# Two feed-forward groups of seven blocks in place of four, and halves of a P V step only where nothing else of TensorE is due shortly

## The chip, the cores and the metric

The kernel runs on one core of a Trainium2 chip. The metric is device time in microseconds (us) of one execution; lower is better. Times given as a median are over the runs shown; a profile is of one execution of its own.

## The reference

A block of a transformer, for 2048 positions of width 512: attention with 32 query heads of 16 dimensions and one key and value head, a feed-forward part of width 1792 with SiLU, and a sigmoid gate that mixes them.

```python
def _A_ref(x, wq, wk, wv, wo):          # H = 32 heads, Dh = 16, S = 2048
    q = (x @ wq).reshape(B, S, H, Dh)   # per head
    k, v = x @ wk, x @ wv               # one head for all
    p = softmax(einsum("bhqd,bkd->bhqk", q, k) * Dh ** -0.5)
    return einsum("bhqk,bkd->bhqd", p, v).reshape(B, S, H * Dh) @ wo
def _B_ref(x, w1, w2):                  # F = 1792
    return silu(x @ w1) @ w2
g = sigmoid((x * gate_w).sum(-1, keepdims=True))
return g * a + (1 - g) * b
```

All inputs are float32, and the kernel keeps nearly that precision: a float32 operand is split into a 16-bit upper and a 16-bit lower part, and a product is made of three passes (upper by upper, upper by lower, lower by upper).

## The kernel before, in words

**Steps.** The queries are worked in 4 chunks `c` of 512 positions and 4 blocks `o` of 8 heads: 16 rounds. A round has 32 steps, one for each 64 keys, so there are 512 steps. A step has two score tiles `S` of 128 x 1024 (TensorE, `scores`, L1225), each turned into probabilities by one exponential of ScalarE (`exponential`, L1231) into a buffer `P` (the rows call it `xs` where the buffer was part of the input's). There are two score buffers, so a score can begin when the exponential before the last one has ended. After the two exponentials the step is multiplied by the values (`pv`, L1262) in one of these ways:
- in 16-bit parts, "A" and "B": VectorE first makes the two lower parts of the step (`low`, L1237, one for each half of the tile, into `L` or `raw`), and TensorE makes a bfloat16 pass and a float16 pass;
- natively in float32, "W": one whole step without VectorE;
- natively in halves, "N" and then "M": the same work as W, in two pieces of 256 columns that other work can stand between.

**The rest of TensorE's work** is one stream of outputs (`Stream`, L851): the blocks of the feed-forward's first product (`ffn_h`, tile `pm` from `xs,w1s`, 12 passes each, 14 blocks for each chunk), its second product (`ffn_o`, from `w2s,H`), the queries (`q_block`, from `xs,wqs`) and the attention's output product (`out_proj`, from `wo_s,O`). TensorE is used as two row halves of 64: an output `new` goes through the lower rows while the output before it, `cur`, goes through the upper rows. Both write their own PSUM bank, of which there are two (`pM`). One such pairing lasts as many passes as the longer of the two and is called a turn here. When `cur` has ended it is evicted (`evict`): the first product through a tanh of ScalarE (L906) and two operations of VectorE (L909, L922), the second product by adding it to the accumulator of its 128 positions (`add_out`, L828 for the first, L830 for the further ones). The next turn waits until that bank is free (`self.last.free`).

**Groups.** The 14 blocks of a chunk are worked in groups (`GROUPS`): the outputs of the second product are made for each group by itself, so each of the 16 tiles of 128 positions gets one addition for each group. The groups of the first three chunks are 4, 3, 4, 3 with the row halves taking different spans (`spans`, `order`), so that 12 passes meet 12 and 9 meet 9; the last chunk has 4, 4, 4, 2, where a turn of 12 meets one of 6. Blocks of the next group are put between the outputs of this one (`mixed`).

**Order.** `attention` writes the order of all engines while the program is built. A planner (`advance`, `pe_next`, `act_next`, `dve_next`) keeps a clock for TensorE, ScalarE and VectorE, with fixed costs (`PASS` 0.216, `HALF` 0.435, `EXP` 0.905 and others), and takes for each engine what is ready and has the lowest priority number. For TensorE a score has 0, a P V step 4 (3 for A and B, 1 when the backlog of steps is long), the stream 2 while it is behind a steady pace and 5 when it is ahead. A whole native step is only taken where the next score would still be in time for ScalarE; where it isn't, but a half would be, the step is begun in halves:

```python
if HALVES and r is not None and s not in left_of and max(r, now["PE"]) > most:
    fits, kind = most + HALF, "NM"
```

VectorE takes a step's lower parts if it can end both within `ROOM` of the first exponential. On the chip each engine follows the order written, and waits only where an operand isn't there.

**Other parts.** Before the loop lies a prologue (keys, first queries, the first pieces of the weights), and the weights are loaded and split in `pieces`, one every 5.6 us by the planner. The last three steps of the last round are made by halves of the queries (L1218, L1250), and four products with the last part of `wo` end the kernel (L1715).

Of the kernel before, what the change touches and what calls it, by code (L numbers as in the profile page):

```python
# [36 lines left out]
HALVES = True  # L37
PAIRS = 3
XUSE = "PPP "
GROUPS = (4, 3, 4, 3), (4, 3, 4, 3), (4, 3, 4, 3), (4, 4, 4, 2)  # L40
UNEVEN = [sum(g) == 14 and g[:3] == (4, 3, 4) for g in GROUPS]
# [15 lines left out]
def kernel(  # L57
# [99 lines left out]
    pieces = [(w1, 0, a) for a in range(KD)]  # L157
    for g in range(len(GF)):
        if g + 1 < len(GF):
            pieces += [(w1, g + 1, a) for a in range(KD)]  # L160
        if g == 0:
            pieces += [(wq, 0, a) for a in range(2)]
        pieces += [(w2, g, a) for a in range(GF[g])]
# [645 lines left out]
    def attention(ctx, pO, scale_of, t_scale, shifts, split_pieces, chores, q_todo, early, gates_, v_bank):  # L809
# [29 lines left out]
        class Out:  # L839


            def __init__(self, terms, ready, kind, evict, add=None, upper=None):
                self.kind, self.evict, self.ready, self.add = kind, evict, ready, add
                parts = lambda terms: [(l, r, i, j) for l, r in terms for i, j in ((0, 0), (0, 1), (1, 0))]
                self.mm = parts(terms)
                self.mm_hi = self.mm if upper is None else parts(upper)
                self.free = self.wait = None
# [16 lines left out]


# [27 lines left out]
        def weights(w, k):  # L893
            _, f0, n_f = blocks[k]
            return all(split_pieces.ready(w, g) for g in range(len(GF)) if f0 < sum(GF[:g + 1]) and f0 + n_f > sum(GF[:g]))

        def ffn_h(k, f):
            c, f0, n_f = blocks[k]
            fa = f0 + f
            f0 = fa * 128  # L900

            def tangent(o, t):
                x_used(c, t)
                e = wp.tile([128, 512], F32, name="e", bufs=EB)
                e_left[0] -= 1
                nc.scalar.activation(e, o.bank, AF.Tanh, scale=t_scale)  # L906
# [21 lines left out]
            return Out([(lambda i, b, m, n=32, kt=kt: w1s[b, i, kt, f0 + m:f0 + m + n],  # L928
                         lambda j, b, kt=kt: xs[b, c, j, kt]) for kt in range(KD)],
                       lambda: 0.0 if weights(w1, k) else None, "h",  # L930
                       lambda o, t: tanhs.append((t, lambda t: tangent(o, t))))

        def spans(k, t):

            c, f0, n = blocks[k]
            g = k % 4
            if not UNEVEN[c]:
                return range(f0, f0 + n), range(f0, f0 + n)
            a, b = ((0, 4, 7, 11, 14), (0, 3, 7, 10, 14))[::1 if t % 2 == 0 else -1]
            return range(a[g], a[g + 1]), range(b[g], b[g + 1])  # L940

        def order(k):

            return (1, 0, 3, 2) if UNEVEN[blocks[k][0]] and k % 2 else (0, 1, 2, 3)

        def ffn_o(k, t):
            c, f0, n_f = blocks[k]
            spans_ = spans(k, t)
            used = sorted({*spans_[0], *spans_[1]})

            def ready():
                if not weights(w2, k) or any((c, f) not in h_done for f in used):
                    return None
                return max(h_done[c, f] for f in used)

            def evict(o, when):
                if t == order(k)[-1]:
                    kept = {f for n in range(4) for q in spans(k + 1, n) for f in q} if k + 1 < len(blocks) and blocks[k + 1][0] == c else set()
                    h_more([Hs.pop((c, f)) for f in range(f0 + n_f) if (c, f) in Hs and f not in kept], when)
                o.added(when)  # L960

            terms = [[(lambda i, b, m, n=32, f=f: Hs[c, f][b, i, t * 128 + m:t * 128 + m + n],
                       lambda j, b, f=f: w2s[b, j, f]) for f in q] for q in spans_]
            return made_out(terms[0], ready, "o", evict, c, t, g1, terms[1])

        def made_out(terms, ready, kind, evict, c, t, gate, upper=None):
            o = Out(terms, ready, kind, evict, upper=upper)
            o.add = lambda: add_out(c, t, o.bank, gate)
            return o
# [82 lines left out]
        def outs():  # L1052

            def mixed(k):
                hs = [lambda f=f: ffn_h(k, f) for f in range(blocks[k][2])] if k < len(blocks) else []
                os_ = [lambda t=t: ffn_o(k - 1, t) for t in order(k - 1)] if k else []
                at_once = 0 if not k else 2 if UNEVEN[blocks[k - 1][0]] else 4 if blocks[k - 1][2] < NF else 1
                for _ in range(len(hs) if k == len(blocks) - 1 else LEAD - 1):
                    if hs:
                        yield hs.pop(0)  # L1060
                while len(hs) > 1 or os_:
                    if len(hs) > 1:
                        yield hs.pop(0)
                    if queue:
                        yield lambda n=queue.pop(0): q_block(n)
                    for _ in range(at_once):
                        if os_:
                            while k and blocks[k - 1][0] > asked[0]:
                                yield None
                            left[0] -= 1  # L1070
                            yield os_.pop(0)
                yield from hs

            for n in early:
                yield q_block(n)
            for k in range(len(blocks) + 1):
                for make in mixed(k):
                    if make is None:
                        yield urgent.pop(0)() if urgent else None
                        continue  # L1080
                    while k == len(blocks) and any((blocks[k - 1][0], f) not in h_done for f in range(14)):
                        yield urgent.pop(0)() if urgent else None
                    yield make()
                    while urgent:
                        yield urgent.pop(0)()
            while True:
                yield urgent.pop(0)() if urgent else None
# [4 lines left out]
        class Stream:  # L1092


            def __init__(self):
                self.new = self.cur = self.last = self.next = None
                self.n = self.i = self.others = self.passes = 0
                self.paired = False

            def ready(self):  # L1100

                if self.i < self.n:
                    return self.new.wait if self.new and not self.i else 0.0
# [4 lines left out]
                if self.last and self.last.free is None:  # L1108
                    return None
                r = self.next.ready()  # L1110
                return None if r is None else max(r, self.last.free if self.last else 0.0)

            def turn(self, t):

                if self.cur and not (self.next and self.paired):
# [3 lines left out]
                if self.new:  # L1119
                    self.new.bank, self.new.wait = pM.tile([128, 512], F32, name="pm"), 0.0  # L1120
                    if any(b[3] <= t for b in bounds):
                        bound(self.new, t + PASS + LATE)
                        return True

            def go(self, t):
                if self.i == self.n and self.turn(t):
                    return
                for m in range(4):
                    if self.new and self.i < len(self.new.mm):
                        self.new.product(self.new.mm[self.i], lo, m, self.i == 0, False)  # L1130
                    k = self.i - self.n + len(self.cur.mm_hi) if self.cur else -1
                    if k >= 0:
                        self.cur.product(self.cur.mm_hi[k], hi_, m, False, self.i == self.n - 1)
                self.i += 1
                self.passes += 1
                if self.i == self.n:
                    self.paired = self.cur is not None
                    if self.cur:
                        self.cur.evict(self.cur, t + PASS + LATE)
                        self.last = self.cur  # L1140
# [435 lines left out]
        def pe_next():  # L1576
# [19 lines left out]
            ok = [x for x in cands if x[0] <= t + 0.03]  # L1596
            return min(ok, key=lambda x: x[1]) if ok else min(cands, key=lambda x: x[0], default=None)
# [90 lines left out]
        while head[0] < len(steps) or left[0] > 4 or tanhs or len(h_done) < sum(GF) * NCH:  # L1688
            advance()
# [75 lines left out]
```

## Time and profile before

| what | value |
|---|---|
| median of 3 runs | 1030.44 us (1029.58 to 1033.46) |
| profiled execution | 1030.14 us, its span 1028.4 us |
| TensorE busy | 1006.5 us (98%) |
| ScalarE busy | 992.3 us (96%) |
| VectorE busy | 924.5 us (90%) |
| GpSimd busy | 60.0 us (6%) |
| exponentials / low parts / additions L830 with `g` | 1024 / 490 / 48 |

A row of a timeline gives start, length, engine, line, operation, output and inputs, and how many instructions are merged in it. Matmuls are pipelined and a row's length reaches to the end of the last one, so the cost of a pass on TensorE is read from its start to the start of what follows. A pass is 8 matmuls, a native half or whole step shows as 16. A row of a group gives the count after the x, then busy time and mean length, then the idle time of the engine before it and what ended it.

### The profile page before, as it was taken

The numbers are of one execution on the slowest core, as the hardware profiler recorded it, in microseconds if no ns is written. First come the engines' busy times: TensorE is split into PE (matmuls) and PEld (weight loads), VectorE is DVE, ScalarE is ACT, GpSimd is POOL, SyncE is SP. The second block draws the span as 40 slices with busy tenths as digits, with TensorE's granted clock in tenths as the row PEclk, the third lists the DMA queues.
The fourth block names the chain that finished last, engine by engine and source line by source line (L and its number), as shares of the span: only waits on it lengthen the run. The fifth ranks groups of instructions, "written<-read, shape, count | busy, mean of one in ns | idle before, by whom it ended". The sixth has DMA issues, their size and how long they took to land.

```text
span 1028.4 us, 69785 instructions
## 1 busy us (share of the span) xinstructions
PE 1006.5 (98%) x32760; PEld 616.2 (60%) x32760; DVE 924.5 (90%) x1199; ACT 992.3 (96%) x1108; POOL 60.0 (6%) x138
## 2 busy tenths in 40 slices
PE   8999999999999999999999999999999999999996
PEld 6456565666655656565656556566666556565563
DVE  7888978989999999999999999899998989999893
ACT  5999999999999999999999999999999999999994
POOL 4101101100000000000000000000000000000000
PEclk9999999999999999999999999999999999999999
DMA  5123322311010111101011010100110110101001
GB/s 208 48 87 85 82 59 60 76 45 25 10 42 18 48 33 25 30 5 32 19 24 41 24 46 15 35 20 15 47 27 17 43 39 10 36 10 19 5 4 47
DMA packets 28115, 40.14 MB, mean 39 GB/s; under 512 B 5689, under 2 KB 19370, under 8 KB 27818
## 3 DMA queue, kind: packets, MB, share of 16 engines
q0 software_dynamic: 10656, 15.73, 7.4%
q1 hardware_dynamic: 16442, 19.27, 5.9%
q8 instruction: 258, 4.23, 1.8%
q10 hardware_dynamic: 720, 0.59, 0.2%
q14 instruction: 39, 0.32, 0.1%
HBM read 19.98 MB, written 8.25 MB: 27 GB/s over the span
## 4 chain that ended last, share of the span: by engine, by line
PE 83%; ACT 10%; DVE 3%; issue 3%; DMA 1%; SPq 0%; ACTq 0%
PE pm L851 32%; PE pv L1262 28%; PE S L1225 20%; ACT P L1231 7%; ACT xs L1231 2%; DVE L L1237 1%; ACT e L906 1%; PE pv L1250 1%; DMA xn<-in_A_x_dram 1%; PE pt L339 0%; DVE xs L132 0%; DVE e L909 0%; PE pv L518 0%; PE pm L436 0%; PE S L1218 0%
## 5 line engine op out<-in xcount | busy, mean ns | idle before, releaser
L1231 ACT ACTIVATE P<-S 128x1024 f32<-128x1024 f32 x770 | 737.5, 1077 | 10.5 <-PE S L1225 5.5
L1225 PE MATMUL S<-qb,KT 50*32 50x512 f16 x8096 | 483.4, 379 | 5.7 <-ACT P L1231 1.8
L1225 PEld LDWEIGHTS <-KT 50*32 50x32 f16 x8096 | 206.1, 90 | 189.1 <-issue 100.0
L1237 DVE TENSOR_TENSOR L<-P 128x1024 f16<-128x1024 f32 x227 | 271.5, 1217 | 20.7 <-ACT P L1231 19.6
L851 PE MATMUL pm<-xs,w1s 64*32 64x512 f16 x5376 | 274.8, 375 | 1.1 <-DVE e L909 0.8
L851 PE MATMUL pm<-w2s,H 64*32 64x512 f16 x5376 | 273.8, 375 | 1.3 <-DVE e L909 0.8
L1262 PE MATMUL pv<-P,VF 64*32 64x256 f32 (+1 forms) x5056 | 267.5, 450 | 0.3
L1231 ACT ACTIVATE xs<-S 128x1024 f32<-128x1024 f32 x254 | 253.6, 1080 | 2.1 <-PE S L1225 0.9
L851 PEld LDWEIGHTS <-w1s 64*32 64x32 f16 x5376 | 126.5, 93 | 44.2 <-issue 8.4
L851 PEld LDWEIGHTS <-H 64*32 64x32 f16 x5376 | 125.3, 93 | 44.0 <-issue 4.3
L1237 DVE TENSOR_TENSOR raw<-P 128x1024 f16<-128x1024 f32 x109 | 131.1, 1218 | 2.3 <-ACT P L1231 2.0
L1262 PEld LDWEIGHTS pv<-P,VF 64*32 64x32 f32 x5056 | 112.1, 106 | 34.3 <-issue 3.3
L1237 DVE TENSOR_TENSOR L<-xs 128x1024 f16<-128x1024 f32 x90 | 108.0, 1218 | 3.9 <-ACT xs L1231 3.4
L1262 PEld LDWEIGHTS <-VP 64*32 64x32 f16 x3920 | 79.5, 92 | 36.0 <-issue 5.5
L851 PE MATMUL pm<-xs,wqs 64*32 64x512 f16 x1440 | 100.3, 375 | 0.1
L1262 PE MATMUL pv<-L,VP 64*32 64x512 f16 x1268 | 92.3, 375 | 0.3 <-DVE L L1237 0.2
L1262 PE MATMUL pv<-P,VP 64*32 64x512 bf16 x1344 | 81.9, 387 | 0.0
L1237 DVE TENSOR_TENSOR raw<-xs 128x1024 f16<-128x1024 f32 x64 | 76.9, 1217 | 2.4 <-ACT xs L1231 2.2
L851 PE MATMUL pm<-wo_s,O 64*32 64x512 f16 x1440 | 75.1, 375 | 0.6 <-issue 0.2
L918 POOL DMA_DIRECT2D H<-e x56 | 30.4, 542 | 729.4 <-DVE e L909 725.2
L1262 PE MATMUL pv<-xs,VF 64*32 64x256 f32 (+1 forms) x1216 | 62.5, 432 | 0.2 <-issue 0.2
L1262 PE MATMUL pv<-raw,VP 64*32 64x512 f16 x692 | 58.3, 375 | 0.0
(215 smaller groups left out, 710.5 us busy)
## 6 DMA issues: line engine op xcount, KB each, us to landing
H<-e POOLq DMA_DIRECT2D x56, 128.0 KB, 2.5
raw<-in_B_w_dram POOLq DMA_DIRECT2D x24, 256.0 KB, 3.3
qb<-qd SPq DMA_DIRECT2D x180, 32.0 KB
xn<-in_A_x_dram SPq DMA_DIRECT2D x8, 512.0 KB
out_dram<-acc SPq DMA_DIRECT2D x14, 256.0 KB
qd<-qx SPq DMA_DIRECT2D x13, 256.0 KB
raw<-in_A_wo_dram POOLq DMA_DIRECT2D x4, 256.0 KB, 3.1
qb<-sh SPq DMA_DIRECT2D x60, 2.0 KB
```

Of the source, the lines that this page charges most:

```text
L851: nc.tensor.matmul(self.bank[32 * m:32 * m + 32], l(i, rows, 32 * m), r(j, rows), start=first, stop=last)
L906: nc.scalar.activation(e, o.bank, AF.Tanh, scale=t_scale)
L918: nc.gpsimd.dma_start(H[:, 0], e)
L1225: nc.tensor.matmul(sc[32 * m:32 * m + 32, f], KT[b:b + 50, k0:k0 + 32], qtile[i][b:b + 50, m // 2, j], start=True, stop=True)
L1231: nc.scalar.activation(probs[s][:, 2 * j:2 * j + 2], banks.pop(p), AF.Exp, scale=scale_of(*rounds[steps[s][0]]))
L1237: nc.vector.tensor_tensor(lows[s, j], probs[s][:, js], upper(probs[s])[:, js], op=OP.subtract)
L1250: nc.tensor.matmul(pvs[i][h][32 * j:32 * j + 32, 256 * q:256 * q + 256], VF[r, NK - 2 * PAIRS + 2 * u + a], probs[s][r, j, 256 * a:256 * a ...
L1262: nc.tensor.matmul(pvs[i][h][32 * j:32 * j + 32, q], a[r], b[r, q], start=k == 0 and n != "B", stop=k == NK - 1 and n in "BMW")
```

## The change

`GROUPS` becomes (7, 7) for every chunk. An output of the second product then has 7 blocks, 21 passes for each row half, and is made as two `Part`s of 4 and 3 blocks (12 and 9 passes); the second output of a pair takes 3 and then 4 blocks in the upper rows, so that 12 still meets 12 and 9 meets 9. Outputs go in pairs: first part of one, first part of the other, second part of one, second part of the other. Only the last part of an output evicts it. Between two parts of one output at least three scores have to be issued (`o.mark + 3`), since both parts write one bank from different row halves. All 7 blocks of a group come ahead of its outputs, and `asides` puts the queries and the output products between them. The pieces of the weights are loaded in the order that this needs. In `pe_next` a native step in halves is not begun while any other work of TensorE is ready within `GAP` = 0.3 us by the planner's clock. The loop now runs until all of the stream is made.

```diff
-HALVES = True
+HALVES, GAP = True, 0.3
-GROUPS = (4, 3, 4, 3), (4, 3, 4, 3), (4, 3, 4, 3), (4, 4, 4, 2)
+GROUPS = (7, 7), (7, 7), (7, 7), (7, 7)
...
+        class Part:
+            def __init__(self, out, n, low, up, ready, passed):
+                self.out, self.kind, self.ready, self.passed = out, out.kind, ready, passed
+                self.begins, self.ends = low[0] == 0, 3 * up[1] == len(out.mm)
+                self.mm, self.mm_hi = (out.mm[3 * a:3 * b] for a, b in (low, up))
...
+        def ffn_pair(k, ts):
+            c, f0, n = blocks[k]
+            m = max(1, (n + 1) // 4)
+            rest = [(n - 4) * (i + 1) // (m - 1) - (n - 4) * i // (m - 1) for i in range(m - 1)]
+            ends_of = lambda sizes: [(sum(sizes[:i]), sum(sizes[:i + 1])) for i in range(m)]
+            first, last = ends_of([n - sum(rest)] + rest), ends_of(rest + [n - sum(rest)])
+            def part(o, t, i):
+                low, up = first[i], (first, last)[t == ts[1]][i]
+                begin_f, end_f = f0 + min(low[0], up[0]), f0 + max(low[1], up[1])
+                def ready():
+                    if i and n_mm[0] < min(o.mark + 3, 2 * len(steps)):
+                        return None
...
-            def mixed(k):
...
+            for k, (c, _, n) in enumerate(blocks):
+                for f in range(n):
+                    yield ffn_h(k, f)
+                    yield from asides()
+                while c > asked[0]:
+                    yield urgent.pop(0)() if urgent else None
+                for ts in (0, 1), (2, 3):
+                    yield from ffn_pair(k, ts)
+                    yield from asides()
...
             ok = [x for x in cands if x[0] <= t + 0.03]
+            new = [x for x in ok if x[2] == "P" and x[3][1] == "NM" and x[3][0] not in left_of]
+            if new and min((x[0] for x in cands if x not in new), default=1e9) < t + GAP:
+                ok = [x for x in ok if x not in new]
+                cands = [x for x in cands if x not in new]
             return min(ok, key=lambda x: x[1]) if ok else min(cands, key=lambda x: x[0], default=None)
...
-        while head[0] < len(steps) or left[0] > 4 or tanhs or len(h_done) < sum(GF) * NCH:
+        while head[0] < len(steps) or left[0] or tanhs or urgent or isinstance(work.next, Part):
             advance()
```

More of the change, by code (lines that the diff above doesn't have):

```diff
@@ L891, in h_more, with weights @@
                 waiting.pop(0)(t)
-        def weights(w, k):
-            _, f0, n_f = blocks[k]
-            return all(split_pieces.ready(w, g) for g in range(len(GF)) if f0 < sum(GF[:g + 1]) and f0 + n_f > sum(GF[:g]))
+        def weights(w, f0, f1):
+            return all(split_pieces.ready(w, g) for g in range(len(GF)) if f0 < sum(GF[:g + 1]) and f1 > sum(GF[:g]))
         def ffn_h(k, f):
@@ L942, in order @@
[L942 to L964, printed above, removed]
@@ L1052, in outs, with asides @@
         def outs():
-            def mixed(k):
[L1055 to L1072, printed above, removed]
+            def asides():
+                if queue and (queue[0] % NO < 2 or split_pieces.ready(wq, 0)):
+                    yield q_block(queue.pop(0))
+                while urgent:
+                    yield urgent.pop(0)()
             for n in early:
                 yield q_block(n)
[L1076 to L1085, printed above, removed]
+            for k, (c, _, n) in enumerate(blocks):
[7 more added lines that the diff above has]
+                    yield from asides()
             while True:
@@ L1102, in ready @@
                 if self.i < self.n:
-                    return self.new.wait if self.new and not self.i else 0.0
+                    return self.new.out.wait if self.new and not self.i else 0.0
                 if self.next is None:
```

81 lines of the change are left out of this document (47 added, 34 removed).

## The prediction

> **What bounds the kernel now.** I read the page's busy times first, then the busy time by stretch, then ScalarE's and TensorE's timelines, then the groups by shape. The busy times name three engines at once, and the stretches say that this holds all along:
>
> ```profile
> PE 1006.5 (98%) x32760; PEld 616.2 (60%) x32760; DVE 924.5 (90%) x1199; ACT 992.3 (96%) x1108; POOL 60.0 (6%) x138
> ```
>
> ```profile
> 300.00:400.00 100.00, 100.00 (x3312) 59.46 (x3303) 95.95 (x103) 99.93 (x111) 1.58 (x3) 1.00 0.12 33
> 900.00:1000.00 100.00, 98.88 (x3359) 58.98 (x3347) 91.71 (x100) 98.70 (x108) 1.94 (x4) 1.00 0.05 10
> ```
>
> Busy time counts an operation's latency, which overlaps the next one, so full rows don't yet say full engines. The timelines give the step from start to start. ScalarE first:
>
> ```profile
> 25.74 1.94 ACT L1231 ACTIVATE P<-S 128x1024 f32<-128x1024 f32 x2 [0.49 <-PE S L1225]
> ...
> 602.07 3.80 ACT L1231 ACTIVATE P<-S 128x1024 f32<-128x1024 f32 x4
> 605.68 0.67 ACT L906 ACTIVATE e<-pm 128x512 f32<-128x512 f32 x1
> 606.15 3.86 ACT L1231 ACTIVATE P<-S 128x1024 f32<-128x1024 f32 x4
> ...
> 1013.65 1.94 ACT L1231 ACTIVATE P<-S 128x1024 f32<-128x1024 f32 x2
> ```
>
> Four exponentials and the tanh behind them: from 602.07 to 605.68 is 3.61 us, 0.903 for each; the tanh takes 605.68 to 606.15, 0.47. The 1024 exponentials and 56 tanhs would thus fill 924.7 + 26.3 = 951 us. They take from 25.74 to 1015.59, 989.9 us. So ScalarE loses 39 us inside the loop, and 25.7 us ahead of it and 12.8 us behind it are not touched by the change. TensorE's costs stand in a stretch that also holds a boundary between two turns of the stream, whose last pass starts at 392.22 and whose next one at 394.48, and in two later places:
>
> ```profile
> 392.22 0.41 PE L851 MATMUL pm<-w2s,H 64*32 64x512 f16 x8
> 392.44 0.42 PE L1262 MATMUL pv<-P,VP 64*32 64x512 bf16 x8
> 392.68 0.41 PE L1262 MATMUL pv<-xs,VP 64*32 64x512 bf16 x8
> 392.91 0.41 PE L1225 MATMUL S<-qb,KT 50*32 50x512 f16 x8
> 393.12 0.41 PE L1262 MATMUL pv<-raw,VP 64*32 64x512 f16 x8
> 393.34 0.63 PE L1262 MATMUL pv<-P,VF 64*32 64x256 f32 x16
> 393.83 0.41 PE L1225 MATMUL S<-qb,KT 50*32 50x512 f16 x8
> 394.04 0.63 PE L1262 MATMUL pv<-P,VF 64*32 64x256 f32 x16
> 394.48 0.38 PE L851 MATMUL pm<-xs,w1s 64*32 64x512 f16 x1
> ...
> 432.49 1.23 PE L1262 MATMUL pv<-P,VF 64*32 64x512 f32 x16
> 433.35 0.59 PE L1225 MATMUL S<-qb,KT 50*32 50x512 f16 x8
> ...
> 434.26 1.21 PE L851 MATMUL pm<-w2s,H 64*32 64x512 f16 x32
> 435.12 0.56 PE L1225 MATMUL S<-qb,KT 50*32 50x512 f16 x8
> ```
>
> By starts: A 0.24 us (392.44 to 392.68), B and a score 0.22, a half 0.44 (394.04 to 394.48), a whole native step 0.86 (432.49 to 433.35), a pass of the stream 0.86 / 4 = 0.215. The counts are in the busy time of the stream's line and in the groups of native matmuls:
>
> ```profile
> 0.00:1028.40 1028.40, 547.41 (x13632) 255.78 (x13632) 1.00 0.15 39
> ```
>
> ```profile
> L1262 PE MATMUL pv<-P,VF 64*32 64x256 f32 x3296 | 145.9, 375 | 0.2
> L1262 PE MATMUL pv<-P,VF 64*32 64x512 f32 x1760 | 123.4, 589 | 0.1
> L1262 PE MATMUL pv<-xs,VF 64*32 64x256 f32 x896 | 38.8, 375 | 0.0
> L1262 PE MATMUL pv<-xs,VF 64*32 64x512 f32 x320 | 23.8, 590 | 0.2 <-issue 0.2
> ```
>
> That is 13632 / 8 = 1704 passes of the stream, (3296 + 896) / 32 = 131 steps in halves and (1760 + 320) / 16 = 130 whole ones; the 490 low parts below make 245 steps in A and B. TensorE's work in the loop: 1704 x 0.215 = 366, 1024 scores x 0.22 = 225, 131 x 0.88 + 130 x 0.86 = 227, 245 x 0.46 = 113; some 931 us of 990. Neither engine is full: TensorE has 6% and ScalarE 4% over, and what is lost lies between them. A score that stands late in TensorE's order makes ScalarE wait, and TensorE then waits for a score buffer or for a step. So a microsecond less work on TensorE should be worth up to one, and no single wait carries the time.
>
> **The change part by part.** (1) *Additions.* Each of 16 tiles gets two additions fewer, 32 in all. VectorE's groups, with the busy time of all low parts between them:
>
> ```profile
> L830 DVE SCALAR_TENSOR_TENSOR acc<-pm,g,acc 128x512 f32<-128x512 f32 x48 | 35.8, 746 | 11.9 <-PE pm L851 11.7
> L1237 DVE TENSOR_TENSOR L<-P 128x1024 f16<-128x1024 f32 x227 | 271.5, 1217 | 20.7 <-ACT P L1231 19.6
> ```
>
> ```profile
> 0.00:1028.40 1028.40, 577.08 (x490) 1.00 0.15 39
> ```
>
> 32 x 0.746 = 23.9 us of VectorE. By itself it is off the path; but the planner spends VectorE's free time on low parts, two of 1.217 us for a step, so 23.9 / 2.43 = 9.8 steps could change from native to A and B. Each saves TensorE 0.86 - 0.46 = 0.40 us. Bounds: 0 (VectorE is 90% busy, so time it has may go unused as some does now) and -3.9 us. I take 8 steps, -3.2 us, nearer to the upper end, since VectorE is 92 and 96% busy in the two stretches shown.
>
> (2) *Uneven turns.* In the last chunk four outputs of 6 passes stand between ones of 12: two turns have 6 passes with only one row half at work. With 12 meeting 12 and 9 meeting 9 these 6 + 6 half passes become 6 whole ones: 6 x 0.215 = -1.3 us. The bound on the other side is 0, if those passes fell in TensorE's waits.
>
> (3) *Parts.* Two parts of one output need three scores between them: 2 for each pair, 16 pairs, 32 places, where the stream stands still. It stands still at a turn's end now too, until the bank is free: at the boundary above for 394.48 - 392.44 = 2.0 us, with two scores in it, and every gap between them is filled with steps. Where a part would have waited for two scores, it now waits for a third, 393.83 - 392.91 = 0.92 us longer. At worst TensorE has only the score in that time: 32 x (0.92 - 0.22) = +22 us. At best steps fill all of it, and no eviction is waited for at these places: 0, or a little below. The boundary shown is filled, so I take +1.0. What the wait holds up is the stream alone; scores and steps pass it in the planner's order. The Trainium skill, "TensorEngine Tiling (Array Packing)", section "Gotcha 1: PSUM Pressure", says that different row tiles cannot access one PSUM bank at once and that software must keep them apart. No row of before shows two row halves on one bank; by that rule the wait could not be left out, and its price is the one bounded here.
>
> (4) *Halves.* Two halves cost 0.88 and a whole step 0.86, so changing one for the other is worth 131 x 0.02 = 2.6 us of TensorE at most. The rule changes the order: with the stream ready, its passes of 0.215 fill the gap ahead of a score, and native steps are kept for the boundaries. A half that stands in front of a score costs ScalarE time here:
>
> ```profile
> 579.28 0.81 PE L1262 MATMUL pv<-P,VF 64*32 64x256 f32 x16
> 579.74 0.58 PE L1225 MATMUL S<-qb,KT 50*32 50x512 f16 x8
> ...
> 580.37 1.02 ACT L1231 ACTIVATE xs<-S 128x1024 f32<-128x1024 f32 x1 [0.40 <-PE S L1225]
> ```
>
> By 579.28 the stream had a few passes left to run, and the score came up 0.46 us later than it could have. ScalarE's idle time by the groups bounds what can be had:
>
> ```profile
> L1231 ACT ACTIVATE P<-S 128x1024 f32<-128x1024 f32 x770 | 737.5, 1077 | 10.5 <-PE S L1225 5.5 <-PE pv L1262 1.3 <-PE S L1218 0.9
> L1231 ACT ACTIVATE xs<-S 128x1024 f32<-128x1024 f32 x254 | 253.6, 1080 | 2.1 <-PE S L1225 0.9 <-PE S L1218 0.5
> ```
>
> 12.6 us, of which this place is 0.40. On the other side, a step kept back leaves TensorE idle for up to 0.3 us each time: 131 x 0.3 = +39. I take -2.4, a fifth of the 12.6: far from the +39, because the stream is ready for most of the time and fills what a half leaves.
>
> (5) *Edits at nothing.* The order of the weights' pieces and seven blocks in a row ahead of their outputs: 7 x 12 = 84 passes at 1.7 for each score are some 50 us, in which the second product's weights arrive by the planner's pace; if that cover fails, the stream stands still once, at the start, for up to one piece (5.6 us). The last of seven blocks is due two turns before the second parts need it, about 11 us, against a tanh, two VectorE operations and this copy:
>
> ```profile
> H<-e POOLq DMA_DIRECT2D x56, 128.0 KB, 2.5
> ```
>
> The outputs' DMAs and the copies on GpSimd keep their number. In the last microseconds the products with `wo` stay as they are; the feed-forward was inside the loop before and remains there.
>
> Sum: -3.2 - 1.3 + 1.0 - 2.4 = -5.9 us. The profiled execution took 1030.14 us (span 1028.4 and 1.7 around it), 0.3 below the median of 1030.44: 1024.5 on the median.
>
> **Rivals.** *A: no change.* VectorE's 24 us are spent on nothing (by `ROOM`, 3.6 us less two low parts of 1.15, VectorE must be free within 1.3 us of a step's first exponential, and the freed time may not lie there) and the order by halves is worth nothing: -1.3 + 1.0, and with a few steps -1 more: 1029. For it: VectorE's 20.7 us of idle time before low parts wait for ScalarE, not for VectorE. Against it: the rest of VectorE's time is taken. A page of the Trainium skill points the same way: "Perfetto Trace Analysis", section "Identifying the Most-Contended Engine", takes the share of weight loads and not of matmuls for TensorE's distance from its limit. By that rule TensorE has 40% over, the most-contended engine is ScalarE, which the change doesn't relieve, and the time stays at 1030; the trace disagrees so far as starts follow each other at 0.215 us whenever work is there.
>
> *B: slower, native steps kept back.* There are 4 `P` buffers in the first chunk. If the stream is always ready, a step that just misses its place for a whole native step is kept back until the backlog fills the buffers; then ScalarE waits for `pv` and not for `S`. Today that wait is 1.3 us in all (the row above). It decides from 5.9 / 0.3 = 20 full waits of 0.3 us. With half of the 131 places at 0.2 us it is +13, and the time 1024.5 + 2.4 + 13 = 1040 with the gain of (4) gone too. Against it: at the boundaries, where the stream isn't ready, halves remain allowed.
>
> *C: the rule hardly bites*, since most halves are begun at boundaries already: (4) falls away, 1027.
>
> **How the numbers follow.** A measurement of this kernel tells about 0.5%, 5 us, from no change. The forecast has 0.42, A and C together 0.36 (A 0.24, C 0.12), B, or the worse half of (3), 0.22. Faster by over 0.5%, below 1025.3: the forecast's 0.42 and a few hundredths of C, where more low parts come than I took, less those of the forecast that fall short: 0.44. Same: 0.36. Slower, above 1035.6: 0.20. The forecast's own range is 1018 to 1027: at the lower end (1) and (2) at their full value, 5.2, and half of the 12.6 of (4). The whole range takes in A and half of B: 1016 to 1037.
>
> **What would show it.** (1): the additions with `g` at L830 from 48 to 16, and low parts from 490 to about 506; right additions with 490 low parts is A. (3): the boundaries between rows of `w2s,H` with three scores or more in them, and TensorE without idle time there. (4): far fewer than 4192 matmuls of 64x256 with `VF`, more of 64x512, and ScalarE's idle time below 12.6. B: ScalarE's waits for `pv` above 1.3, or gaps on TensorE before scores. The forecast is wrong if TensorE's work falls by 5 us and the span from first to last exponential stays at 990: then the loss is in the order, and not in the work.

## The result: 1021.9 us, 0.9% faster, and the profile after

The changed kernel takes 1021.89 us (median of 6 runs, 1021.03 to 1023.51), the kernel before 1032.08 (6 runs, 1029.58 to 1033.78). The ratio is 0.9908, with a 95% interval of 0.9892 to 0.9923: by the ratio some 9.5 us less (the medians are 10.2 apart), where 5.9 were forecast. Each profiled execution lies within 2 us of its median: 1022.62 with a span of 1020.8, against 1030.14 with 1028.4.

In the changed kernel the exponential is at L1230, the scores at L1224, `pv` at L1261, the stream at L848, the low parts at L1236 and the additions at L825 and L827. The busy times on its page:

```profile
PE 998.8 (98%) x31528; PEld 590.4 (58%) x31528; DVE 913.9 (90%) x1177; ACT 987.1 (97%) x1108; POOL 59.4 (6%) x138
```

TensorE has 1232 matmuls fewer (32760 before), VectorE 10.6 us less. The span in stretches, up to the first exponential, to the last one's end, and behind it; the columns are stretch, length, then busy time and count of PE, PEld, DVE, ACT and POOL, clock, DMA share and GB/s. First the kernel before:

```profile
25.70:1015.60 989.90, 979.63 (x32500) 597.64 (x32500) 898.83 (x1130) 977.76 (x1081) 49.27 (x90) 1.00 0.14 34
1015.60:1028.40 12.80, 4.94 (x32) 1.79 (x32) 5.46 (x12) 0.00 (x0) 0.00 (x0) 0.87 0.25 88
```

and the changed one:

```profile
25.40:1007.50 982.10, 971.57 (x31247) 571.40 (x31255) 887.73 (x1107) 972.59 (x1081) 48.62 (x90) 1.00 0.14 34
1007.50:1020.80 13.30, 5.36 (x64) 2.35 (x48) 5.91 (x13) 0.04 (x1) 0.00 (x0) 0.90 0.24 85
```

The stretch from the first exponential to the end of the last one is called the loop below, what follows it the tail. All of the gain between these two executions lies in the loop (7.8 us), and the clock is full in both loops. The 1024 exponentials and 56 tanhs are the same, so ScalarE loses 31.1 us above its 951 in place of 38.8. The groups by shape of the changed kernel (count, busy time and mean length, idle time and what ended it):

```profile
L1230 ACT ACTIVATE P<-S 128x1024 f32<-128x1024 f32 x776 | 741.2, 1094 | 9.3 <-PE pv L1261 3.7 <-PE S L1224 3.7 <-ACT P L1230 0.3
L1230 ACT ACTIVATE xs<-S 128x1024 f32<-128x1024 f32 x248 | 246.7, 1097 | 0.7 <-PE S L1224 0.3
L1261 PE MATMUL pv<-P,VF 64*32 64x512 f32 x2448 | 166.9, 589 | 0.1
L1261 PE MATMUL pv<-P,VF 64*32 64x256 f32 x1440 | 58.7, 375 | 0.0
L1261 PE MATMUL pv<-xs,VF 64*32 64x512 f32 x784 | 52.8, 589 | 0.0
L1261 PE MATMUL pv<-xs,VF 64*32 64x256 f32 x288 | 11.6, 375 | 0.0
L827 DVE SCALAR_TENSOR_TENSOR acc<-pm,g,acc 128x512 f32<-128x512 f32 x16 | 12.0, 751 | 4.7 <-PE pm L848 4.3
```

and the busy time of the low parts over the span:

```profile
0.00:1020.80 1020.80, 589.36 (x500) 1.00 0.15 39
```

Native steps: (1440 + 288) / 32 = 54 in halves (131 before) and (2448 + 784) / 16 = 202 whole (130); 500 low parts make 250 steps in 16 bits (245). ScalarE's idle time by the groups fell from 12.6 to 10.0 us: 4.0 for scores (6.4), but 3.7 for `pv` (1.3). TensorE's timeline shows what now stands between two scores while the stream is ready:

```profile
408.77 0.41 PE L1224 MATMUL S<-qb,KT 50*32 50x512 f16 x8
408.99 0.38 PE L848 MATMUL pm<-xs,wqs 64*32 64x512 f16 x1
...
409.64 0.41 PE L1224 MATMUL S<-qb,KT 50*32 50x512 f16 x8
...
410.50 0.42 PE L1224 MATMUL S<-qb,KT 50*32 50x512 f16 x8
...
411.37 0.41 PE L1224 MATMUL S<-qb,KT 50*32 50x512 f16 x8
411.59 1.06 PE L1261 MATMUL pv<-P,VF 64*32 64x512 f32 x16
412.45 0.41 PE L1224 MATMUL S<-qb,KT 50*32 50x512 f16 x8
```

Scores start 0.87 apart; the rows left out are three passes of the stream in each gap. Then a native step goes in whole, and that score starts 1.08 us on. A stop between two parts of the second product, from the pass at 291.13 to the one at 293.87:

```profile
291.13 0.41 PE L848 MATMUL pm<-w2s,H 64*32 64x512 f16 x8
291.34 0.42 PE L1261 MATMUL pv<-xs,VP 64*32 64x512 bf16 x8
291.83 0.41 PE L1224 MATMUL S<-qb,KT 50*32 50x512 f16 x8
292.05 1.05 PE L1261 MATMUL pv<-P,VF 64*32 64x512 f32 x16
292.91 0.41 PE L1224 MATMUL S<-qb,KT 50*32 50x512 f16 x8
293.13 0.41 PE L1261 MATMUL pv<-raw,VP 64*32 64x512 f16 x8
293.66 0.41 PE L1224 MATMUL S<-qb,KT 50*32 50x512 f16 x8
293.87 0.84 PE L848 MATMUL pm<-w2s,H 64*32 64x512 f16 x24
```

With the pass itself, two 16-bit passes, three scores and a whole native step, 6 x 0.22 + 0.86 = 2.18 of the 2.74 us are filled. No exponential is late there; ScalarE's rows at this place:

```profile
289.82 4.71 ACT L1230 ACTIVATE P<-S 128x1024 f32<-128x1024 f32 x5
294.34 2.02 ACT L1230 ACTIVATE xs<-S 128x1024 f32<-128x1024 f32 x2
```

Five in 4.52 us are 0.904 for each.

### The profile page after: what moved, and what is told of

Its sections match the earlier page's. It is cut to its first block, busy times and chain, and to the rows that moved or that the text cites. A ratio compares the mean times of both kernels' runs of the same rounds, so it can differ in the third digit from the quotient of the medians.

```text
span 1020.8 us, 67262 instructions
## 1 busy us (share of the span) xinstructions
PE 998.8 (98%) x31528; PEld 590.4 (58%) x31528; DVE 913.9 (90%) x1177; ACT 987.1 (97%) x1108; POOL 59.4 (6%) x138
## 4 chain that ended last, share of the span: by engine, by line
PE 48%; issue 24%; ACT 17%; DVE 6%; DMA 3%; POOL 1%; SPq 0%; ACTq 0%; POOLq 0%; DVEq 0%
PE pm L848 19%; PE pv L1261 15%; ACT P L1230 12%; PE S L1224 12%; ACT xs L1230 4%; DVE L L1236 2%; DMA raw<-in_B_w_dram 1%; ACT e L909 1%; DVE raw L1236 1%; DMA H<-e 1%; POOL raw L190 1%; DVE e L912 1%; PE pv L1249 1%; DMA xn<-in_A_x_dram 1%; POOL H L921 0%
## 5 line engine op out<-in xcount | busy, mean ns | idle before, releaser
L1230 ACT ACTIVATE P<-S 128x1024 f32<-128x1024 f32 x776 | 741.2, 1094 | 9.3 <-PE pv L1261 3.7
L1224 PE MATMUL S<-qb,KT 50*32 50x512 f16 x8096 | 447.2, 379 | 7.5 <-ACT P L1230 3.5
L1224 PEld LDWEIGHTS <-KT 50*32 50x32 f16 x8096 | 203.2, 89 | 226.3 <-issue 134.0
L1236 DVE TENSOR_TENSOR L<-P 128x1024 f16<-128x1024 f32 x248 | 296.6, 1219 | 28.9 <-ACT P L1230 25.2
L848 PE MATMUL pm<-xs,w1s 64*32 64x512 f16 x5376 | 258.0, 375 | 0.9 <-DVE e L912 0.9
L1230 ACT ACTIVATE xs<-S 128x1024 f32<-128x1024 f32 x248 | 246.7, 1097 | 0.7 <-PE S L1224 0.3
L848 PE MATMUL pm<-w2s,H 64*32 64x512 f16 x5376 | 240.0, 375 | 0.8 <-DVE e L912 0.3
L1261 PE MATMUL pv<-P,VF 64*32 64x512 f32 (+1 forms) x3888 | 225.4, 510 | 0.1
L1236 DVE TENSOR_TENSOR raw<-P 128x1024 f16<-128x1024 f32 x126 | 151.4, 1219 | 6.4 <-ACT P L1230 6.1
L848 PEld LDWEIGHTS <-w1s 64*32 64x32 f16 x5376 | 116.8, 93 | 45.3 <-issue 6.0
L848 PEld LDWEIGHTS <-H 64*32 64x32 f16 x5376 | 112.7, 93 | 43.4 <-issue 4.8
L848 PE MATMUL pm<-xs,wqs 64*32 64x512 f16 x1440 | 101.3, 375 | 0.2
L1236 DVE TENSOR_TENSOR L<-xs 128x1024 f16<-128x1024 f32 x78 | 93.5, 1218 | 4.9 <-ACT xs L1230 4.6
L1261 PEld LDWEIGHTS <-VP 64*32 64x32 f16 x4000 | 75.2, 93 | 34.8 <-issue 4.3
L1261 PEld LDWEIGHTS pv<-P,VF 64*32 64x32 f32 x3888 | 79.6, 106 | 20.6 <-issue 2.4
L1261 PE MATMUL pv<-L,VP 64*32 64x512 f16 x1304 | 88.4, 375 | 0.1
L1261 PE MATMUL pv<-P,VP 64*32 64x512 bf16 x1496 | 83.3, 387 | 0.0
L848 PE MATMUL pm<-wo_s,O 64*32 64x512 f16 x1440 | 66.3, 375 | 0.1
L1261 PE MATMUL pv<-xs,VF 64*32 64x512 f32 (+1 forms) x1072 | 64.4, 531 | 0.0
L1236 DVE TENSOR_TENSOR raw<-xs 128x1024 f16<-128x1024 f32 x48 | 57.9, 1217 | 4.7 <-ACT P L1230 2.1
L1261 PE MATMUL pv<-raw,VP 64*32 64x512 f16 x696 | 55.2, 375 | 0.0
```

The source lines that it names most:

```text
L848: nc.tensor.matmul(self.bank[32 * m:32 * m + 32], l(i, rows, 32 * m), r(j, rows), start=first, stop=last)
L1224: nc.tensor.matmul(sc[32 * m:32 * m + 32, f], KT[b:b + 50, k0:k0 + 32], qtile[i][b:b + 50, m // 2, j], start=True, stop=True)
L1230: nc.scalar.activation(probs[s][:, 2 * j:2 * j + 2], banks.pop(p), AF.Exp, scale=scale_of(*rounds[steps[s][0]]))
L1236: nc.vector.tensor_tensor(lows[s, j], probs[s][:, js], upper(probs[s])[:, js], op=OP.subtract)
L1261: nc.tensor.matmul(pvs[i][h][32 * j:32 * j + 32, q], a[r], b[r, q], start=k == 0 and n != "B", stop=k == NK - 1 and n in "BMW")
```

## The experiments

All twelve in one table. They ran on three chips, each beside the kernel before, which took 1031.84 us with the first four, 1033.66 with the next four and 1024.60 with the last four; the record doesn't name the chip of the result itself. "Steps" are whole native / in halves / 16-bit; "left" is how many passes of the stream follow the last score (for e1 by the planner, since its trace lacks 48 of the stream's 13632 matmuls); loop and tail are from the profiled execution.

| run | steps | left | loop, tail us | median us | ratio to before, 95% |
|---|---|---|---|---|---|
| before | 130 / 131 / 245 | 0 | 989.9, 12.8 | 1032.08 | 1 |
| changed | 202 / 54 / 250 | 0 | 982.1, 13.3 | 1021.89 | 0.9908 (0.9892 to 0.9923) |
| e1: before, rule alone | 223 / 48 / 235 | 15 | 988.9, 14.8 | 1030.93 | 0.9995 (0.9982 to 1.0008) |
| e2: changed, no rule | 129 / 130 / 247 | 0 | 991.1, 13.1 | 1027.07 | 0.9951 (0.9934 to 0.9969) |
| e3: changed, additions put back | 222 / 44 / 240 | 0 | 984.3, 14.4 | 1026.34 | 0.9952 (0.9933 to 0.9971) |
| e4: before, fewer additions | 131 / 121 / 254 | 0 | 992.4, 13.0 | 1033.07 | 1.0012 (0.9990 to 1.0034) |
| e5: before, `START` 0.4 | 130 / 131 / 245 | 0 | 992.7, 12.8 | 1032.85 | 0.9992 (0.9971 to 1.0013) |
| e6: changed, `START` 0.4 | 202 / 54 / 250 | 0 | 981.6, 12.5 | 1022.85 | 0.9896 (0.9867 to 0.9925) |
| e7: changed, `GAP` 0.6 | 262 / 0 / 244 | 62 | 979.3, 31.2 | 1039.01 | 1.0059 (1.0041 to 1.0078) |
| e8: changed, rule only from the second chunk | 196 / 70 / 240 | 3 | 983.2, 15.0 | 1025.51 | 0.9921 (0.9894 to 0.9947) |
| e9: before, rule and fewer additions | 209 / 54 / 243 | 3 | 980.5, 13.7 | 1024.66 | 1.0001 (0.9991 to 1.0011) |
| e10: changed, `GAP` 0.2 | 163 / 89 / 254 | 0 | 990.3, 13.7 | 1030.30 | 1.0048 (1.0031 to 1.0065) |
| e11: changed, six scores between parts | 191 / 66 / 249 | 103 | 979.6, 42.9 | 1050.94 | 1.0262 (1.0246 to 1.0277) |
| e12: before, `TANH_DONE` 0.70 | 138 / 123 / 245 | 0 | 981.8, 12.6 | 1022.54 | 0.9978 (0.9966 to 0.9989) |

**e1, the rule alone in the old groups.**

```diff
-HALVES = True
+HALVES, GAP = True, 0.3
...
             ok = [x for x in cands if x[0] <= t + 0.03]
+            new = [x for x in ok if x[2] == "P" and x[3][1] == "NM" and x[3][0] not in left_of]
+            if new and min((x[0] for x in cands if x not in new), default=1e9) < t + GAP:
+                ok = [x for x in ok if x not in new]
+                cands = [x for x in cands if x not in new]
```

> The kernel before with the rule on halves alone (GAP = 0.3), groups of 4, 3, 4, 3 as they were. Theory 'order' (late scores behind halves cost the time): the steps in halves fall from 131 to some 60, the time from the first exponential to the last by 3 to 6 us, the time to about 1027. Theory 'work' (VectorE's 24 us turn into steps in 16-bit parts): VectorE's additions stay at 48 with g, so the time stays within 2 us of before.

Worth nothing by itself. ScalarE's groups in this run, which read 5.5 for scores and 1.3 for `pv` before:

```profile
L1231 ACT ACTIVATE P<-S 128x1024 f32<-128x1024 f32 x778 | 741.4, 1078 | 12.4 <-PE S L1225 5.5 <-PE pv L1262 4.7 <-ACT P L1231 0.7
```

Waits for `pv` rose to 4.7, there are 10 fewer 16-bit steps, and the stream ends late:

```profile
25.40:1014.30 988.90, 975.57 (x31055) 567.02 (x31056) 873.76 (x1107) 973.93 (x1081) 48.83 (x90) 1.00 0.14 34
1014.30:1029.10 14.80, 8.71 (x112) 3.68 (x106) 7.44 (x15) 0.04 (x1) 0.00 (x0) 0.92 0.22 78
```

The loop gains 1 us and the tail loses 2. The waits for `pv` are rival B's sign, but the changed kernel has 3.7 us of them and gains all the same; and 10 steps that went from 16 bits to native are 10 x 0.40 = 4 us more work of TensorE, of which 83 fewer steps in halves give back 83 x 0.02 = 1.7. What eats the rule's gain here wasn't separated.

**e2, the groups of seven without the rule.** The four lines of e1's second hunk are taken out of the changed kernel.

> The changed kernel without the rule on halves: groups of seven alone. Theory 'order': steps in halves are back at about 130 and 3 to 6 us are given back, 1025 to 1028. Theory 'work': the 16 additions with g and some 500 low parts stay, and so does the time, within 2 us of the changed kernel.

0.9951: about half of the gain is the groups' (5 us), the rest, 0.9951 to 0.9908 or 4.4 us, comes with the rule; the two intervals don't overlap. (The two ratios may come from different chips; the kernel before took 1031.8 and 1032.1 beside them.) Its profiled execution took 1031.6, 4.5 above its median, so its counts are safer than its times: 247 steps in 16 bits, 130 in halves, much as before the change. In it ScalarE's largest group waits for scores more than before (5.5):

```profile
L1230 ACT ACTIVATE P<-S 128x1024 f32<-128x1024 f32 x766 | 732.9, 1073 | 10.9 <-PE S L1224 7.6 <-PE pv L1261 0.8 <-ACT P L1230 0.3
```

**e3, the additions put back into the changed kernel.** A further operation of the same size behind each addition with `g1`, with the planner told of it and the bank free at the same time.

```diff
+            if gate is g1:
+                nc.vector.scalar_tensor_tensor(a, a, 0.0, a, op0=OP.mult, op1=OP.add)
...
-                    self.free = t
+                    self.free = t - more
-                task(t, t, 0.67, run, True)
+                more = 0.67 if self.kind == "o" else 0.0
+                task(t, t, 0.67 + more, run, True)
```

> The changed kernel with 32 more operations of VectorE of about 0.7 us each, right behind the additions of the feed-forward (acc = acc * 0 + acc on the accumulator, so that the output is the same); the planner counts them, and the PSUM bank is still free after the first one. VectorE's load is then as before. Theory 'work': low parts fall from 500 to about 490 and the time rises by 2 to 4 us. Theory 'order': within 1 us of the changed kernel.

By the ratios, with the same reservation as for e2, 4.5 us of the gain go: 240 steps in 16 bits in place of 250, the busy time of the low parts is

```profile
0.00:1024.10 1024.10, 565.89 (x480) 1.00 0.15 39
```

In the prediction's prices the step counts of e3 are 3.8 us more work of TensorE than those of the changed kernel, so here the time follows the work.

**e4, fewer additions in the old groups.** Two of four groups of each chunk are evicted without their addition.

```diff
-                o.added(when)
+                if k % 4 in (1, 2):
+                    o.free = when + 0.8
+                else:
+                    o.added(when)
```

> The kernel before with the additions of the second and third group left out (32 of 64; that part of the feed-forward is missing from the output), the planner taking the bank as free at the same time as before. Theory 'work': VectorE's 24 us give 5 to 10 more steps in 16-bit parts and 2 to 4 us. Theory 'order': halves stay at about 130 and the time within 1 us of before.

The freed time of VectorE is used, as in term (1) of the prediction: 508 low parts, 9 more steps in 16 bits, and VectorE as busy as before (923.3 against 924.5).

```profile
0.00:1030.50 1030.50, 596.93 (x508) 1.00 0.15 39
```

TensorE has 9 x (0.88 - 0.46) = 3.8 us less work. The time does not move: 1.0012, with 0.9990 as the lower end of its interval, 1 us less at most.

**e5 and e6, the same two kernels with another constant of the planner** (`START` 0.3 to 0.4 in each).

> The kernel before with one number of the planner's clock changed that has to do with no theory: the first score is thought ready at 0.4 us in place of 0.3 (START). The order after it comes out another one, with the same rules. It measures how far the time moves by the luck of an order alone: within 2 us of before if differences of 4 us are to be believed, 4 us or more off if they are not.

> The same change of START in the changed kernel: within 2 us of the changed kernel (1022) if its gain is of its rules, nearer to before if part of it is the luck of one order.

The numbers of steps came out unchanged, so these are repeats more than new orders: 1032.85 and 1022.85, ratios 0.9992 and 0.9896. They don't tell how much of the gain is luck of one order, but the gain came again: 1.0% on their chip.

**e7, the limit at 0.6** (`GAP` 0.3 to 0.6 in the changed kernel).

> The changed kernel with the limit GAP at 0.6 us in place of 0.3: a half is begun only where TensorE has nothing else for 0.6 us. Theory 'order' in its simple form: fewer halves still, fewer late scores, 1020 to 1022. Rival 'kept back': the exponentials' waits for a P buffer, 4.7 us in the changed kernel, rise by 3 us or more and the time to 1025 or above.

No step is begun in halves any more, and the loop is shorter than the changed kernel's. But the stream is not done at its end:

```profile
25.70:1005.00 979.30, 962.78 (x29900) 541.21 (x29904) 871.75 (x1090) 971.60 (x1081) 48.64 (x90) 1.00 0.14 34
1005.00:1036.20 31.20, 21.49 (x551) 10.55 (x535) 9.54 (x19) 0.00 (x1) 0.00 (x0) 0.94 0.11 39
```

```profile
1015.90 10.19 PE L848 MATMUL pm<-w2s,H 64*32 64x512 f16 x288 [0.88 <-DVE acc L827]
```

and the groups show that ScalarE didn't wait much longer for buffers than in the changed kernel (3.7):

```profile
L1230 ACT ACTIVATE P<-S 128x1024 f32<-128x1024 f32 x776 | 739.8, 1092 | 7.0 <-PE pv L1261 3.8 <-PE S L1224 2.1 <-ACT P L1230 0.3
```

The loop is shorter by 2.8 us, but 62 x 0.215 = 13 us of the stream are not in it: TensorE had more unused time there than in the changed kernel, not less. The work comes back behind the loop, with nothing of ScalarE's beside it, and the tail is 17.9 us longer.

**e8, the rule only from the second chunk on**, where there are more than 4 `P` buffers (`if new and n_bufs[0] > 4 and ...`).

> The changed kernel with the rule on halves only from the second chunk on, where there are 5 to 7 P buffers in place of 4. Theory 'kept back' (the rule makes steps wait and ScalarE wait for a P buffer while there are four): the waits for a buffer in the first 300 us fall from 4.7 to about 1.5 us and the time to about 1019. Rival (the late scores of the first chunk are worth as much as the buffer waits): within 2 us of the changed kernel.

```profile
L1230 ACT ACTIVATE P<-S 128x1024 f32<-128x1024 f32 x768 | 733.1, 1080 | 7.1 <-PE S L1224 4.4 <-PE pv L1261 0.6 <-ACT P L1230 0.3
```

Most waits for `pv` are gone (0.6 for 3.7), so they were the first chunk's, as rival B has it. But the time isn't better (1025.51). The order also has 10 fewer steps in 16 bits, 16 more in halves and 3 passes left over, so what the 3 us of waits were worth can't be read from it.

**e9, the rule and fewer additions in the old groups** (the edits of e1 and e4 together).

> The kernel before with both the rule on halves (0.3) and the 32 additions left out (that part of the feed-forward is missing from the output), in the old groups of 4, 3, 4, 3. Its order has 54 steps in halves, 243 in 16-bit parts and 3 passes of the stream behind the last score (the rule alone: 48, 235 and 15). Theory 'together' (the rule delays steps and costs low parts unless VectorE has time; the groups of seven only give that time): 7 to 9 us less than before, 1022 to 1025. Rival 'parts' (what counts is how the stream is cut into turns of two-part outputs): within 3 us of before.

```profile
25.70:1006.20 980.50, 972.98 (x31215) 565.83 (x31222) 869.59 (x1091) 972.07 (x1081) 48.87 (x90) 1.00 0.14 34
1006.20:1019.90 13.70, 6.66 (x95) 3.07 (x78) 7.17 (x17) 0.01 (x1) 0.00 (x0) 0.89 0.23 84
```

Its profile, of the fastest of its 12 runs (1021.69), looks like the changed kernel's, in steps and in loop, and its median is 1024.66. But on that chip the kernel before took 1024.60, 7 to 9 us less than on the others, and the ratio is 1.0001. So the two parts together give nothing measurable there without the groups. What the changed kernel would take on that chip wasn't run.

**e10, the limit at 0.2.**

> The changed kernel with the limit at 0.2 us. Its order has 89 steps in halves in place of 54, and 254 in 16-bit parts in place of 250. Theory 'late scores alone' (every half put in front of a score costs): between no rule (1027) and 0.3 (1022), 1023 to 1025. Rival 'balance' (a longer limit buys fewer late scores with longer buffer waits): 1020 to 1022, and the buffer waits below 3 us.

0.5% slower than before on that chip, with 254 steps in 16 bits and 89 in halves. None of the accounts here expects it. The granted clock in its profile is 0.995, the lowest of the fourteen (0.995 to 0.997 in its six runs, 0.998 or 0.999 in those of the kernel before beside it). If the time went with the clock, that would be 3 or 4 us at most, an estimate; the rest stays open.

**e11, six scores between two parts** (`o.mark + 3` to `o.mark + 6`).

> The changed kernel with six scores in place of three between two parts of one output: the wait doubled at 32 places. Its order puts 103 passes of the stream behind the last score (none in the changed kernel). If steps fill the wait, as the prediction had it at +1 us for the first score, the loop keeps its length but the stream falls behind: 103 x 0.215 = 22 us and the turns' waits among them at the end, 1045 to 1055. If the wait were idle TensorE time, the loop itself would grow by up to 32 x 3 x 0.7 = 67 us.

```profile
26.00:1005.60 979.60, 958.95 (x30630) 544.41 (x30634) 879.34 (x1096) 970.67 (x1079) 47.75 (x88) 1.00 0.14 34
1005.60:1048.50 42.90, 30.54 (x880) 15.34 (x863) 12.15 (x24) 1.19 (x2) 1.06 (x2) 0.96 0.13 36
```

The longer wait doesn't hold up ScalarE: the loop is among the shortest. But it isn't filled either. 103 x 0.215 = 22 us of the stream are not in this loop, and it is only 2.5 us shorter than the changed kernel's, so by these numbers some 19 us of TensorE's time there went unused, 0.6 us for each of the 32 places. The 103 passes are left for the tail, and the kernel is 2.6% slower.

**e12, another order of the old kernel** (`TANH_DONE` 0.67 to 0.70).

> The kernel before with TANH_DONE at 0.70 in place of 0.67 us in the planner: a number without a theory, which does give another order (138 whole steps, 123 in halves, 245 in parts, against 130, 131, 245). The luck of an order: within 2 us of before if differences of 4 us are to be believed.

0.2% faster than before by a constant that only moves the planner's clock, 8 halves fewer: a change of order alone can be worth about 2 us. Its trace is the only one of the old groups, without rule and with all additions, on the chip where the kernel before takes 1024.6, and ScalarE waits there for scores little more than in the changed kernel (3.6 + 0.8 us, against 4.0; 6.4 in the profile of before), with 123 steps in halves:

```profile
L1231 ACT ACTIVATE P<-S 128x1024 f32<-128x1024 f32 x770 | 734.7, 1081 | 6.7 <-PE S L1225 3.6 <-PE pv L1262 1.2 <-ACT P L1231 0.3
L1231 ACT ACTIVATE xs<-S 128x1024 f32<-128x1024 f32 x254 | 253.4, 1096 | 1.1 <-PE S L1225 0.8
```

So steps in halves needn't make scores late.

## Why the prediction was right, and where its sizes were not

**Direction, place and range held, the mechanism in part.** The gain lies between the first and the last exponential, with fewer halves and less idle time of ScalarE; 1021.9 is within 1018 to 1027, the forecast's own range. The sum was too small by 3.6 us. But 5.5 of the 7.7 us that ScalarE loses less lie behind stops of TensorE that the prediction didn't know (last section), so that the sum came this near is partly luck. Point by point:

- *(1) Additions, -3.2.* The step that failed is "a microsecond less work on TensorE should be worth up to one". In e4 the count came as forecast (9 steps for 8) and the time stood still: the prediction's own sign of a wrong forecast, less work and an unchanged span, is the picture of e4. In the changed kernel only 5 more steps went to 16 bits, yet with the additions put back (e3) 4.5 us are lost. So the term's sum was about right inside the new groups and is zero in the old ones; it is not a price for a step. Rival A's outcome, no change, is right for the old order, but not its reason: VectorE's freed time was not spent on nothing, the low parts used it.
- *(3) Parts, +1.0.* The place shown is filled but for 0.56 us, without a late exponential. Twice the wait is not filled: in e11 some 19 us of TensorE's time go unused, where the prediction's bound for the third score alone was 22. What the prediction did not have is where the price falls: not on the loop, but on a stream that must still end. With three scores it ends in time (no pass left); with six it doesn't.
- *(4) Halves, -2.4.* The mis-sized term: the rule is worth 4.4 us in the groups of seven (from ratios that may be of two chips), where it was priced at a fifth of ScalarE's idle time by the groups. The time that ScalarE loses from start to start is the larger measure: 23.9 us behind late scores before, 14.4 after (the steps between all exponentials, less 0.904, or 0.477 behind a tanh). Of the 9.5 us, 2.7 came back as longer waits for a free buffer, 2.0 to 4.7. That is rival B's sign, at a fifth of its price.
- *Groups.* (1), (2) and (3) together were -3.5; e2 has -5.0 for them, without the rule. (2) was not tested by itself.
- *Rival B* came true at 0.6 (e7: 1.0059), but through the stream, not through ScalarE's buffers, which the prediction had named as the place. By e7's rows it is the stream that pays for the steps kept back, behind the loop.
- *The page's rule behind rival A* ("Perfetto Trace Analysis" of the Trainium skill, section "Identifying the Most-Contended Engine", which judges TensorE's headroom by the share of weight loads, and also by its share of peak FLOPs) had the time stay at 1030. The time fell by 0.9%. The weight loads' share was 60% before, where the prediction's sum by starts has TensorE at 931 of 990 us, 94%: here their share by itself doesn't show how near TensorE is to its limit.

**The row shown for (4) was misread.** The prediction read a late score at 579.74 as the half's fault. The rows of TensorE just ahead of it in the kernel before, which it left out:

```profile
578.64 0.37 PE L851 MATMUL pm<-wo_s,O 64*32 64x512 f16 x1
578.64 0.37 PE L851 MATMUL pm<-w2s,H 64*32 64x512 f16 x1
579.26 0.39 PE L851 MATMUL pm<-wo_s,O 64*32 64x512 f16 x1 [0.25 <-issue]
```

A pass of the stream stops among its matmuls for 0.62 us, released by nothing that the profile shows, and goes on. The exponential started 0.40 us late, so by these rows the score would have been in time without the stop, half or not. Such stops are the subject of the last section: ScalarE loses 5.5 us less behind them in the changed kernel, more than (4) had for all halves; whether fewer halves are the reason is open.

**What stays open.** The parts don't add: rule alone 0, additions alone 0, groups with their fewer additions 5, all three 9.5. On the third chip, the rule with fewer additions (e9) equals the kernel before, which itself is faster there. Whether the changed kernel keeps its 0.9% on that chip is not known; its nearest relative there, e10, is slower than the kernel before.

## What to carry to other kernels

When two engines are both nearly full and feed each other, price an edit by what it does to late starts on the engine that sets the pace, not by the work that it removes; the same work was worth nothing in one order (e4) and 4.5 us in another (e3). Work that fills gaps must still end with the loop: look for what is left behind the last item (e7, e11) before a longer wait or a stricter rule is called free. Before a late operation is blamed on the instruction ahead of it, look whether that engine stood still in the middle of a group that has nothing to wait for.

## What the runs showed of the hardware

**TensorE stops where nothing is awaited, about 1.1 us ahead of an instruction packet.** An example in the kernel before, in the middle of the eight matmuls of one score:

```profile
461.02 0.38 PE L1225 MATMUL S<-qb,KT 50*32 50x512 f16 x1
461.03 0.38 PE L1262 MATMUL pv<-P,VF 64*32 64x256 f32 x1
461.94 0.41 PE L1225 MATMUL S<-qb,KT 50*32 50x512 f16 x7 [0.54 <-issue]
```

The next packet of the instruction queue starts at 463.08, 1.14 us behind the stop's end. Counting stops of over 0.45 us (start to start, from 26 to 1000 us) without a releaser: 19 before, 16 of which end 0.98 to 1.93 us ahead of such a packet, though packets are 3.8 us apart in the median; 4 after. The queue's rows, of before and of after (packets, MB, share of the DMA engines' time):

```profile
q8 instruction: 258, 4.23, 1.8%
```

```profile
q8 instruction: 248, 4.06, 1.6%
```

The 4 us ahead of a stop hold 277 records of TensorE's matmuls and weight loads, against 263 on average before and 255 after. What ScalarE loses from the start of such a stop to 2 us behind it is 6.8 us before and 1.3 after: 5.5 of the 7.7 us by which its loss fell. In the 14 kernels the stops' sum goes with the loop's length (correlation 0.86): 9.6 to 12.4 us of stops where the loop takes 990 or more, 2.0 to 5.1 where it takes 979 to 985, with e1 (5.6 us and 988.9) beside the line and e10 (4.9 and 990.3) off it. A half has as many instructions as a whole step in about half the time, so fewer halves make a thinner stream of instructions; that this is the cause was only argued, since no run changed the instructions without the order.

The other traces bear out the stops and weaken this reason. e5 and e6, the same pair again on one chip, have 21 and 5 stops (12.4 and 2.6 us). But e12, with 123 steps in halves and nearly as many matmuls as before (32632), has only 9 (5.1 us), on the chip where the kernel before is 7 us faster than beside e1 to e4. So the stops seem to depend on the chip as well, and part of the gain may be had only where the kernel before has many of them; no trace of the kernel before was taken on that chip.

**One kernel's time differs between chips by 0.9%.** The kernel before took 1031.8, 1033.7 and 1024.6 us beside the three sets of runs, at a granted clock of 0.998 or 0.999 in each run. That is as much as the whole change, so each run is compared with the kernel before beside it, and a gain of this size is known only for the chips on which it was run.
